# Weight-block sums moved from GpSimd to VectorE, two slices per tile, and more products kept for the end, in a two-layer mixture-of-experts kernel

## The chip, the cores and the metric

The kernel runs on one core of a Trainium2 chip. The metric is the device time of one execution in microseconds (us). TensorE is PE in the profile (PEld its weight loads), VectorE is DVE, ScalarE is ACT, GpSimd is POOL, and SP is the engine whose queue issues most DMAs.

## The reference, cut to what matters

Attention and a dense gated layer come first and yield x (2304 tokens x 512). Then each token goes to 2 of 8 experts:

```
out = zeros((2304, 512))
for e in range(8):
    for k in range(2):
        mask = top2[:, k] == e
        h = maximum(x[mask] @ w1[e], 0.0)                  # w1[e]: 512 x 1024
        out[mask] += top2_w[mask, k, None] * (h @ w2[e])   # w2[e]: 1024 x 512
```

All of it is fp32. The kernel gets that precision by splitting each operand into a rounded high part and a low rest, and using three matmuls per product (high x high, high x low, low x high). The high part is an ACT copy, the low part a DVE subtraction of two tiles in SBUF (the on-chip memory).

## The kernel before, in words

Three stretches follow each other. Up to some 435 us come attention and the dense layer (`slot1`), whose last block also routes the tokens and scatters their rows to DRAM, by expert. Then 32 *units* (some 435 to 549 us) do experts 0 and 1: `up2` is x @ w1 for one slice of 128 hidden columns, `down2` adds its product with w2 to accumulators in PSUM, one unit later. Part "a" of an expert is its first 384 rows, part "b" the rest. Units 12 to 15 are the second half of expert 1, part "a"; unit 16 starts its part "b". The rows of part "b" are loaded by SP (`load_x`, from unit 10 on, but only after the last scatters have landed), transposed by DVE (`trans_x`) and split (`split_x2`). `prep2` splits the weights of a unit two units ahead on ACT and DVE.

From 549 us on come 24 *pairs*, p = 0 to 23, four for each expert 2 to 7. A pair is two slices of w1 and w2. `pair` computes its x @ w1 by seven block products instead of eight (Winograd's form: A11, S2, A12, S3, S1, A22, S4 of the rows times blocks and sums of blocks of the weights); a product is six matmuls of 308 columns (`product`, L1058). The seven results are put together by DVE additions (`u2` L1096, `v` L1103, `y22` L1112, `y21` L1115, `y12` L1122), with ACT for `s1` and the relu, and DVE for the low parts (`split_low`, L1076). The matmuls of a pair with w2 (`down_s`, L1072: 5 row tiles x 2 slices x 3) are done in the next pair, between its products, by `first` and `second`.

For the next pair, each pair also prepares the weights. The raw blocks `wb` (512 KB a slice) stand in four buffers with the tag X1. `sums_ws` forms the sums of blocks, C and D, on GpSimd with four instructions of 256 columns (L1020 to L1023). `high_ws`/`low_ws` (L1038, L1042) split A, B, C and D; `high_w2`/`low_w2` (L1046, L1049) split the w2 part, once per slice. Rows of the next expert are prepared over its predecessor's four pairs: `load_xs` (L969), `trans_xs` (L981), `sums_xs` on GpSimd (L987 to L991), `high_xs`/`low_xs` (L1001, L1005).

The order of all this is written out by hand. `put` and `at` hang a piece of work on a stretch and a position in it; `run` emits all pieces up to a position. Each engine's queue is in order, so a waiting instruction holds all behind it on its engine. In pair p, `first(0)` follows position 1, `first(1)` position 3, `second(0)` and `second(1)` stand at the end (before positions 5 and 6.9).

At the end of an expert `finish` scales an accumulator (row tile t) and `add` adds it to `out` by an indirect DMA on POOL's queue. For the last expert `gather` reads the rows of `out` back in pair 23, `finish` adds on DVE (L928), and `add` scatters the sums; each scatter waits for the one before to land. In pair 23 some `down_s` matmuls of pair 22 are held back for the end (row tiles 3 and 4).

Of the kernel before, what the change touches and what calls it, by code (L numbers as in the profile page):

```python
# [24 lines left out]
E = 8  # L25
# [42 lines left out]
def moe_program(ctx, tc, phi, kv, q, wa, wgn, nz, wb, out):  # L68
# [298 lines left out]
    def places(first):  # L367


        def pt(tag, n, shape=()):  # L370
            pool = w1pool if tag[0] == "G" else wpool
            return pool.tile([128, *shape, 2, 2, 256], F32, tag=tag, name="pt", bufs=n)

        if first:
            t = [pt("X1", 4) for _ in range(4)] + [pt("GH", 2) for _ in range(2)] + [pt("GL", 2) for _ in range(2)]
# [636 lines left out]
    def sums_ws(p):  # L1012
        f0, f1 = WB[24 + 2 * p][:, :512], WB[25 + 2 * p][:, :512]
        if p:
            c, d = [pools["s2"].tile([128, DM], F32, tag=t, name="ts") for t in ("tc", "td")]
        else:
            c, d = ro_tile(), ro_tile()
        TS[p, "C"], TS[p, "D"] = c, d
        u, v = slice(0, 256), slice(256, 512)
        G.tensor_sub(c[:, u], f1[:, u], f0[:, u])  # L1020
        G.tensor_sub(c[:, v], f1[:, v], f1[:, u])
        G.tensor_sub(d[:, u], f1[:, v], c[:, u])
        G.tensor_sub(d[:, v], f0[:, v], d[:, u])  # L1023
# [20 lines left out]
    def high_w2(n):  # L1044
        W2[n] = wtile()
        A.activation(r(W2[n][:, 0]), WB[n][:, 512:], AF.Copy)  # L1046

    def low_w2(n):
        V.tensor_sub(r(W2[n][:, 1]), WB[n][:, 512:], W2[n][:, 0])  # L1049
# [12 lines left out]
    def down_s(p, n, tiles):
        e, f = 2 + p // 4, 2 * (p % 4) + n
        hh, hl = HS[p, n]
        w = W2[24 + 2 * p + n]
        for t in tiles:
            h = height(e, t)
            if f == 0:
                AC2[e, t] = bank((0, 1, 4, 2, 3)[t], [128, DM], "acc")
            o = slice(128 * t, 128 * t + h)  # L1070
            for m, (a, b) in enumerate(((hh, 0), (hh, 1), (hl, 0))):
                P.matmul(AC2[e, t][:h], r(a[:, o]), r(w[:, b]), start=(f == 0 and m == 0),  # L1072
                         stop=(f == NF2 - 1 and m == 2))
# [4 lines left out]
    def pair(p, first, second):  # L1078
        e = 2 + p // 4
        lo, hi = slice(0, HB), slice(HB, CAPS)  # L1080

        def temp(name):
            return pools["s2"].tile([128, HB], F32, tag=name, name=name)

        h0 = [act.tile([128, CAP], F32, tag=t, name="hs") for t in ("ah", "al")]
        HS[p, 0] = h0
        run(("s", p), 0)
# [37 lines left out]
        run(("s", p), 6.9)  # L1125
        split_low(h1[1][:, lo], y12, h1[0][:, lo])
# [25 lines left out]
    for n in range(4):  # L1152
        put(last, 2 * n + 3.5, load_wb, n)
# [40 lines left out]
    for k in range(4):  # L1194
        then_x(1, 4 + k, "a", 1, k, "b")
# [21 lines left out]
    then(2, 1, "b", 0.5, sums_ws, 0)  # L1217
# [3 lines left out]
    then(2, 6, "b", 2.2, high_w2, 24)  # L1221
# [4 lines left out]
    pairs = 4 * (E - 2)  # L1226
    for p in range(pairs):
        e, q = 2 + p // 4, p % 4
        n = 24 + 2 * p
        at(p, 0, high_w2, n + 1)  # L1230
        at(p, 0, low_w2, n)
        at(p, 1, load_wb, n + 4)
        at(p, 2, low_w2, n + 1)
        at(p, 3, load_wb, n + 5)
        if p + 1 < pairs:
            at(p, 0, sums_ws, p + 1)
            for h, g, k in ((1, 2, "A"), (3, 4, "B"), (3, 5, "C"), (5, 6, "D")):
                at(p, h, high_ws, p + 1, k)
                at(p, g, low_ws, p + 1, k)
            at(p, 6, high_w2, n + 2)  # L1240
        if e + 1 < E:
            if q == 0:
                at(p, 0, load_xs, e + 1)
            if q == 2:
                at(p, 5.5, index, e + 1, "ab")
            for h, fn, k, m in {0: ((5.1, trans_xs, 0, 0), (5.1, trans_xs, 0, 1), (6.1, sums_xs, 0, 0)),
                                1: ((1.1, high_xs, 0, 0), (2.1, low_xs, 0, 0), (1.2, high_xs, 0, 1),
                                    (2.2, low_xs, 0, 1), (3.1, high_xs, 0, 2), (4.1, low_xs, 0, 2),
                                    (4.2, sums_xs, 0, 1), (5.2, high_xs, 0, 3), (6.1, low_xs, 0, 3)),
                                2: ((2.1, trans_xs, 1, 0), (4.1, trans_xs, 1, 1), (5.2, sums_xs, 1, 0),  # L1250
                                    (5.2, high_xs, 1, 0), (6.1, low_xs, 1, 0)),
                                3: ((1.1, high_xs, 1, 1), (2.1, low_xs, 1, 1), (1.2, high_xs, 1, 2),
                                    (2.2, low_xs, 1, 2), (2.3, sums_xs, 1, 1), (5.2, high_xs, 1, 3),
                                    (6.1, low_xs, 1, 3))}[q]:
                at(p, h, fn, e + 1, k, m)
    then(2, 4, "b", 1, index, 2, "ab")
# [20 lines left out]
    for p in range(pairs):  # L1277
        e, q = 2 + p // 4, p % 4
        at(p, 2.5, add)
        at(p, 5.9, add)  # L1280
# [9 lines left out]
        else:  # L1290
            ends, held = q == 0, p == pairs - 1

            def first(h):
                down_s(p - 1, 0, (range(3), range(3, 3 if held else NC))[h])

            def second(h):
                t = (range(1), range(1, 3)) if held else (range(3), range(3, NC))
                down_s(p - 1, 1, t[h])
                if ends:
                    finish(e - 1, t[h])  # L1300
# [96 lines left out]
```

## Time and profile before

| what | us |
|---|---|
| median of 3 runs (lowest, highest) | 894.87 (894.37, 895.64) |
| the profiled execution | 897.11 |
| its span in the trace | 895.3 |
| PE busy, share | 837.7, 94% |
| PEld busy, share | 735.6, 82% |
| DVE busy, share | 644.1, 72% |
| ACT busy, share | 394.5, 44% |
| POOL busy, share | 336.1, 38% |

PE's busy time has modelled ends; idle time of PE is what the stretches, the waits and the timeline show.

### The profile page before, as it was taken

How to read it: one execution, taken by the hardware profiler on the slowest of the kernel's cores; microseconds unless marked ns; L12 is line 12 of the kernel's file. 1: busy time of each engine (PE TensorE's matmuls, PEld its weight loads, DVE VectorE, ACT ScalarE, POOL GpSimd, SP SyncE). 2: the span in 40 equal slices, each digit the busy share in tenths (PEclk: the TensorE clock that was granted, in tenths of full speed). 3: DMA queues.
4: the chain of work that ended last, by engine and by line, in shares of the span. 5: the costliest groups of instructions: out<-in, count | busy, mean ns of one | idle time of the engine just before them, and what ended most of it. 6: DMA issues, size and time to landing. Idle time of an engine off the chain costs nothing.

```text
span 895.3 us, 16500 instructions
## 1 busy us (share of the span) xinstructions
PE 837.7 (94%) x6136; PEld 735.6 (82%) x6136; DVE 644.1 (72%) x1498; ACT 394.5 (44%) x845; POOL 336.1 (38%) x443
## 2 busy tenths in 40 slices
PE   5898999999999999999997999899999999999992
PEld 2676888899989999898876878788888888888881
DVE  4786587776767685858673665788889989888751
ACT  4663555343443243334342544445454454544520
POOL 2000012424242333432223154545738557475622
PEclk9998999999999999999999999899999999999997
DMA  9965729875336443467466955455475645653431
GB/s 320 400 247 196 208 97 302 262 242 142 106 84 212 119 126 88 127 211 188 151 202 167 202 157 85 117 128 133 92 157 116 139 118 120 127 130 102 86 79 59
DMA packets 85082, 142.02 MB, mean 159 GB/s; under 512 B 16432, under 2 KB 41232, under 8 KB 84992
## 3 DMA queue, kind: packets, MB, share of 16 engines
q1 hardware_dynamic: 65712, 100.66, 36.8%
q0 software_dynamic: 19280, 40.22, 19.5%
q8 instruction: 50, 0.82, 0.4%
q14 instruction: 40, 0.33, 0.1%
HBM read 104.07 MB, written 36.77 MB: 157 GB/s over the span
## 4 chain that ended last, share of the span: by engine, by line
PE 65%; DVE 13%; DMA 11%; issue 5%; ACT 3%; POOL 1%; SPq 1%; DVEq 0%; POOLq 0%; ACTq 0%
PE acc L459 13%; PE acc L1072 12%; PE ph L1058 11%; PE pg L426 9%; PE pv L426 7%; DMA xs<-R,gidx 4%; PE ph L896 3%; PE acc L914 3%; PE acc L455 2%; PE pp L314 2%; DVE ws L1049 2%; DVE xh L1005 2%; DMA out<-pv,ix 1%; DVE ws L1042 1%; PE pT L481 1%
## 5 line engine op out<-in xcount | busy, mean ns | idle before, releaser
L1072 PE MATMUL acc<-ws,hs 128*128 128x512 f32 (+1 forms) x720 | 183.1, 396 | 0.0
L1058 PE MATMUL ph<-xh,ws 128*128 128x308 f32 x1008 | 165.0, 308 | 10.2 <-DVE ws L1042 4.4
L1058 PEld LDWEIGHTS ph<-xh,ws 128*128 128x128 f32 x1008 | 152.3, 189 | 25.7 <-DVE ws L1042 6.1
L1072 PEld LDWEIGHTS acc<-ws,hs 128*128 128x128 f32 (+1 forms) x720 | 129.5, 186 | 25.7
L459 PE MATMUL acc<-a,ro 128*128 128x288 f32 x576 | 116.3, 295 | 0.0
L426 PE MATMUL pg<-x,pt 128*128 128x288 f32 x576 | 103.9, 316 | 6.5 <-ACT pt L394 4.7
L459 PE MATMUL acc<-a,os 128*128 128x288 f32 x432 | 105.9, 294 | 0.8 <-DVE os L408 0.8
L938 POOL DMA_INDIRECT out<-pv,ix x40 | 65.1, 1629 | 109.0 <-ACT pv L931 57.9
L426 PEld LDWEIGHTS pg<-x,pt 128*128 128x128 f32 x576 | 83.0, 193 | 24.8 <-issue 6.2
L426 PE MATMUL pv<-x,pt 128*128 128x288 f32 x576 | 94.0, 299 | 0.0
L459 PEld LDWEIGHTS acc<-a,ro 128*128 128x128 f32 x576 | 92.2, 188 | 0.0
L439 DVE SCALAR_TENSOR_TENSOR ta<-ta,pg 128x288 f32<-128x288 f32 x84 | 37.8, 450 | 66.5 <-ACT ta L434 66.5
L426 PEld LDWEIGHTS pv<-x,pt 128*128 128x128 f32 x576 | 83.8, 193 | 0.0
L622 POOL DMA_INDIRECT xs<-R,gidx x48 | 49.0, 1021 | 88.4 <-DMA xs<-R,gidx 83.2
L418 POOL DMA_DIRECT2D os<-osl x72 | 40.6, 564 | 106.1 <-PE acc L459 62.0
L459 PEld LDWEIGHTS acc<-a,os 128*128 128x128 f32 x432 | 74.1, 189 | 1.1 <-DVE os L408 1.1
L434 ACT ACTIVATE ta<-pg 128x288 f32<-128x288 f32 x84 | 34.3, 408 | 88.4 <-PE pg L426 88.2
L445 ACT ACTIVATE a<-ta 128x288 fp32r<-128x288 f32 x84 | 37.3, 444 | 73.0 <-DVE ta L440 72.7
L896 PE MATMUL ph<-xt,wm 128*128 128x384 f32 (+1 forms) x256 | 59.1, 318 | 2.3 <-ACT xt L858 1.1
L1076 DVE SCALAR_TENSOR_TENSOR hs<-y,hs 128x308 fp32r<-128x308 f32 x72 | 50.9, 707 | 3.4 <-ACT hs L1123 0.5
L896 PEld LDWEIGHTS ph<-xt,wm 128*128 128x128 f32 x256 | 45.1, 193 | 6.6 <-ACT xt L858 2.2
L896 PE MATMUL ph<-xt,ro 128*128 128x384 f32 (+1 forms) x128 | 40.5, 317 | 5.2 <-DVE ro L779 5.1
(213 smaller groups left out, 1524.1 us busy)
## 6 DMA issues: line engine op xcount, KB each, us to landing
wb<-wb SPq DMA_DIRECT2D x72, 512.0 KB, 4.3
os<-osl POOLq DMA_DIRECT2D x72, 256.0 KB, 3.4
stg<-wa SPq DMA_DIRECT2D x19, 511.8 KB, 7.9
kv<-kv SPq DMA_DIRECT2D x32, 256.0 KB, 5.4
xl<-xs SPq DMA_DIRECT2D x40, 160.0 KB, 6.5
out<-zt SPq DMA_DIRECT2D x1, 5888.0 KB, 24.2
xd<-R SPq DMA_DIRECT2D x8, 603.0 KB, 4.8
qt<-q SPq DMA_DIRECT2D x8, 576.0 KB, 6.5
```

The lines of the kernel that those rows point to most:

```text
L418: G.dma_start(r(lo), r(osl[f][:, :]))
L426: P.matmul(p, r(PT[f // 2, g][:, w, f % 2, 128 * a:128 * a + 128]), r(X[i][:, s, g, :]), start=(g == 0 and n == 0), stop=(g == 1 and n == 2))
L434: A.activation(ta, pg, AF.Tanh, scale=0.5)
L439: V.scalar_tensor_tensor(ta, ta, 1.0, pg, op0=OP.add, op1=OP.mult)
L445: A.activation(r(ah[:, 0, :]), ta, AF.Copy)
L459: P.matmul(ACC[i][c], r(OS[i, f][w][:, o]), r(ah[:, s, :]), start=(f == 0 and n == 0), stop=(f == NF1 - 1 and n == 2))
L622: G.indirect_dma_start(out=xs[:, :], out_offset=bass.IndirectOffsetOnAxis(ap=RT[i][:, t, n:n + 1], axis=0), in_=R[i][:, t, :], in_offset=None)
L896: P.matmul(p, r(w[:, c]), r(x[:, k, b, :]), start=(m == 0), stop=(m == 11))
L938: G.indirect_dma_start(out=out, out_offset=bass.IndirectOffsetOnAxis(ap=IX[e][:h, t:t + 1], axis=0), in_=PV[e, t][:h], in_offset=None, com ...
L1058: P.matmul(out, r(w[:, i, c + 128 * k:c + 128 * k + 128]), r(x[:, m, k, a]), start=(start and n == 0), stop=(n == 5), skip_group_check=not ...
L1072: P.matmul(AC2[e, t][:h], r(a[:, o]), r(w[:, b]), start=(f == 0 and m == 0), stop=(f == NF2 - 1 and m == 2))
L1076: V.scalar_tensor_tensor(r(hl), y, 0.0, hh, op0=OP.max, op1=OP.subtract)
```

## The change

- The four X1 tiles become one tile with four slots; `wb` loads go to slot n % 4. The first four loads stand later in the last dense block.
- `sums_ws` runs on DVE: one subtraction of 512 columns and two of 256. Two stand at position 0 of a pair, the third at 2.
- C and D share a tile for the high and one for the low parts. `high_w2` and `low_w2` do both slices in one instruction; `low_w2` stands at position 2, and both `wb` loads at 3.
- The relu outputs of two slices share a tile: relu and `split_low` of the hi halves become one instruction of 616 columns each. `s1`, `u2` and the y of the hi halves stand in the tiles "ah" and "al".
- All positions of a pair run up to .9 (0.9, 1.9, ...), and there is one more: 6.9 before y12, 7.9 before its `split_low`.
- Rows: part "b" of expert 1 is transposed in units 13 to 15, not 12 to 15. `trans_xs`, `sums_xs`, `high_xs`, `low_xs` have other positions.
- `down_s` products kept for the end: in pair 22 only row tiles 0 and 1 of pair 21 are done, in pair 23 only tile 0 of pair 22. Operands of pair 23 go to an extra tile, KEEP.

```diff
@@ places / load_wb
-            t = [pt("X1", 4) for _ in range(4)] + ...
+            u = pt("X1", 1, (4,))
+            t = [u[:, k] for k in range(4)] + ...
-            WB[n] = wpool.tile([128, 1024], F32, tag="X1", name="wb", bufs=4)
+                WB["all"] = wpool.tile([128, 4, 1024], F32, tag="X1", name="wb", bufs=1)
+            WB[n] = WB["all"][:, n % 4]
@@ sums_ws
-        G.tensor_sub(c[:, u], f1[:, u], f0[:, u])
-        G.tensor_sub(c[:, v], f1[:, v], f1[:, u])
-        G.tensor_sub(d[:, u], f1[:, v], c[:, u])
-        G.tensor_sub(d[:, v], f0[:, v], d[:, u])
+            V.tensor_sub(TS[p][0].rearrange("p (a w) -> p a w", a=2),
+                         raw[:, 1, :DM].rearrange("p (a w) -> p a w", a=2), raw[:, :, u])
+        elif m == 1:
+            V.tensor_sub(TS[p][1][:, u], raw[:, 1, v], TS[p][0][:, u])
         else:
+            V.tensor_sub(TS[p][1][:, v], raw[:, 0, v], TS[p][1][:, u])
@@ high_w2, low_w2 (one call a pair)
+        A.activation(r(W2[p][0]), raw_of(p)[:, :, DM:], AF.Copy)
+        V.tensor_sub(r(W2[p][1]), raw_of(p)[:, :, DM:], W2[p][0])
@@ pair
-        A.activation(r(h1[0][:, hi]), y22, AF.Relu)
-        V.tensor_add(y21, b, s1)
-        A.activation(r(h0[0][:, hi]), y21, AF.Relu)
-        split_low(h1[1][:, hi], y22, h1[0][:, hi])
-        split_low(h0[1][:, hi], y21, h0[0][:, hi])
+        V.tensor_add(y[:, 0], b, s1)
+        A.activation(r(hh[:, :, hi]), y, AF.Relu)
         second(0)
-        run(("s", p), 5)
+        run(("s", p), 5.9)
+        split_low(hl[:, :, hi], y, hh[:, :, hi])
         product(p, c, S4, B22, False)
+        run(("s", p), 6.9)
         V.tensor_add(y12, c, u2)
-        A.activation(r(h1[0][:, lo]), y12, AF.Relu)
+        A.activation(r(hh[:, 1, lo]), y12, AF.Relu)
         second(1)
-        run(("s", p), 6.9)
-        split_low(h1[1][:, lo], y12, h1[0][:, lo])
+        run(("s", p), 7.9)
+        split_low(hl[:, 1, lo], y12, hh[:, 1, lo])
@@ order
-        put(last, 2 * n + 3.5, load_wb, n)
+        put(last, (9.5, 9.6, 11.5, 11.6)[n], load_wb, n)
-        then_x(1, 4 + k, "a", 1, k, "b")
+        put(("u", (13, 14, 14, 15)[k]), (2.2, 1, 2.2, 1)[k], trans_x, 1, k, "b")
+        put(("u", (14, 14, 15, 15)[k]), (0.5, 2.1, 0.5, 2.1)[k], split_x2, 1, k, "b")
-        at(p, 0, low_w2, n)
-        at(p, 1, load_wb, n + 4)
-        at(p, 2, low_w2, n + 1)
+        at(p, 2, low_w2, p)
+        at(p, 3, load_wb, n + 4)
         at(p, 3, load_wb, n + 5)
-            at(p, 0, sums_ws, p + 1)
-            for h, g, k in ((1, 2, "A"), (3, 4, "B"), (3, 5, "C"), (5, 6, "D")):
+            at(p, 0, sums_ws, p + 1, 0)
+            at(p, 0, sums_ws, p + 1, 1)
+            at(p, 2, sums_ws, p + 1, 2)
+            for h, g, k in ((1, 2, "A"), (3, 4, "B"), (3, 5, "C"), (4, 6, "D")):
-            for h, fn, k, m in {0: ((5.1, trans_xs, 0, 0), (5.1, trans_xs, 0, 1), (6.1, sums_xs, 0, 0)),
+            for h, fn, k, m in {0: ((6, trans_xs, 0, 0), (7, trans_xs, 0, 1)),
...
@@ end
+        held = max(0, p - pairs + 3)
+        inline = range((NC, 2, 1)[held])
+                down_s(p - 1, 0, inline[3 * h:3 * h + 3])
...
-    p = pairs - 1
-    down_s(p, 0, range(3))
+    rest = {t: [p for p in range(pairs - 3 + (t < 2) + (t < 1), pairs)] for t in range(NC)}
+    for n in range(2):
+        down_s(rest[1][0], n, (1,))
+    del rest[1][0]
     for t in range(NC):
-        if t > 2:
+        for p in rest[t]:
             for n in range(2):
-                down_s(p - 1, n, (t,))
-            down_s(p, 0, (t,))
-        down_s(p, 1, (t,))
+                down_s(p, n, (t,))
         finish(E - 1, (t,))
```

## Rows read from the trace of the kernel before

**Rows 1.** Busy time by stretch: stretch, length, engines with counts, granted clock, DMA share, GB/s.
```profile
549.00:573.00 24.00, 19.02 (x98) 16.50 (x97) 17.01 (x27) 10.06 (x21) 12.55 (x12) 0.86 0.74 165
...
600.00:654.00 54.00, 52.84 (x290) 45.88 (x289) 47.37 (x74) 27.40 (x57) 32.80 (x30) 1.00 0.59 131
```
**Rows 2.** The same view for two single pairs.
```profile
604.21:617.11 12.90, 12.90 (x73) 11.48 (x72) 9.64 (x18) 7.43 (x16) 3.86 (x3) 1.00 0.59 131
617.11:630.97 13.86, 13.42 (x74) 11.48 (x73) 13.44 (x21) 7.54 (x16) 10.17 (x9) 1.00 0.49 114
```
**Rows 3.** Waits of PEld, 573 to 856 us: waited for, us in total, times, longest.
```profile
PEld ph L1058 <- DVE u L1096: 5.7, 10, 0.7
PEld ph L1058 <- DVE v L1103: 3.4, 8, 0.6
```
**Rows 4.** DVE groups by form, 573 to 816 us (18 pairs): busy, mean ns, idle before.
```profile
L1076 DVE SCALAR_TENSOR_TENSOR hs<-y,hs 128x308 fp32r<-128x308 f32 x54 | 40.1, 742 | 2.1
L1049 DVE TENSOR_TENSOR ws<-wb,ws 128x512 fp32r<-128x512 f32 x36 | 35.5, 986 | 0.0
L1042 DVE TENSOR_TENSOR ws<-ts,ws 128x512 fp32r<-128x512 f32 x36 | 29.3, 813 | 0.0
L1042 DVE TENSOR_TENSOR ws<-wb,ws 128x512 fp32r<-128x512 f32 x18 | 18.7, 1041 | 0.0
...
L1042 DVE TENSOR_TENSOR ws<-wb,ws 128x256 fp32r<-128x256 f32 x18 | 7.8, 435 | 0.0
```
**Rows 5.** The same view, 856 to 896 us, where GpSimd computes nothing.
```profile
L1076 DVE SCALAR_TENSOR_TENSOR hs<-y,hs 128x308 fp32r<-128x308 f32 x5 | 2.4, 477 | 0.8 <-ACT hs L1123 0.5
L1049 DVE TENSOR_TENSOR ws<-wb,ws 128x512 fp32r<-128x512 f32 x2 | 1.4, 712 | 0.0
```
**Rows 6.** One of GpSimd's four groups of sums, 549 to 896 us.
```profile
L1022 POOL TENSOR_TENSOR ts<-wb,ts 128x256 f32<-128x256 f32 x23 | 29.9, 1302 | 3.5 <-DVE ws L1042 3.5
```
**Rows 7.** Timeline of the end: start, us, engine, line, operation, count [idle before, releaser].
```profile
867.68 11.26 PE L1072 MATMUL acc<-ws,hs 128*128 128x512 f32 x48
...
872.05 2.13 DVE L928 SCALAR_TENSOR_TENSOR pv<-acc,ml,pv 128x512 f32<-128x512 f32 x3 [2.68 <-PE acc L1072]
873.08 1.02 POOL L938 DMA_INDIRECT out<-pv,ix  x1 [8.26 <-DVE pv L928]
...
878.98 0.75 DVE L928 SCALAR_TENSOR_TENSOR pv<-acc,ml,pv 104x512 f32<-104x512 f32 x1 [2.02 <-PE acc L1072]
...
887.17 1.01 POOL L938 DMA_INDIRECT out<-pv,ix  x1 [2.59 <-DMA out<-pv,ix]
```
**Rows 8.** Timeline of units 14 and 15 (484 to 498 us), PE, DVE and SP.
```profile
484.49 1.80 SPq L844 DMA_DIRECT2D xl<-xs  x4
484.91 0.52 PE L896 MATMUL ph<-xt,wm 128*128 128x384 f32 x2
...
489.48 0.45 DVE L853 STREAM_TRANSPOSE xu<-xl 128x256 f32<-128x256 f32 x1 [9.49 <-DMA ml<-xs]
...
490.55 0.69 PE L896 MATMUL ph<-xt,ro 128*128 128x384 f32 x1 [5.13 <-DVE ro L779]
...
493.77 0.39 PE L914 MATMUL acc<-wm,hh 128*128 128x512 f32 x1
...
497.96 0.39 PE L914 MATMUL acc<-wm,hh 128*128 128x512 f32 x1
```
**Rows 9.** Timeline of pairs 0 and 1, PE and DVE.
```profile
548.80 1.84 PE L1058 MATMUL ph<-xh,ws 128*128 128x308 f32 x12
...
561.00 1.57 DVE L981 STREAM_TRANSPOSE xr<-xl 128x640 f32<-128x640 f32 x2 [1.92 <-issue]
...
563.20 1.40 PE L1058 MATMUL ph<-xh,ws 128*128 128x308 f32 x4 [4.38 <-DVE ws L1042]
...
571.53 1.86 PE L1058 MATMUL ph<-xh,ws 128*128 128x308 f32 x12
```
**Rows 10.** Loads of weight blocks (L765), 540 to 640 us, issue to landing.
```profile
DMA to landing us min/median/max: 3.1/4.3/7.4
```

More of the change, by code (lines that the diff above doesn't have):

```diff
@@ L374, in places @@
         if first:
-            t = [pt("X1", 4) for _ in range(4)] + [pt("GH", 2) for _ in range(2)] + [pt("GL", 2) for _ in range(2)]
+            u = pt("X1", 1, (4,))
+            t = [u[:, k] for k in range(4)] + [pt("GH", 2) for _ in range(2)] + [pt("GL", 2) for _ in range(2)]
         else:
@@ L763, in load_wb @@
         if n < len(STAGES) * NF2:
-            WB[n] = wpool.tile([128, 1024], F32, tag="X1", name="wb", bufs=4)
+            if "all" not in WB:
+                WB["all"] = wpool.tile([128, 4, 1024], F32, tag="X1", name="wb", bufs=1)
+            WB[n] = WB["all"][:, n % 4]
             Q.dma_start(WB[n], wb[STAGES[n // NF2], n % NF2])
@@ L1042, in low_ws, with high_w2, low_w2 @@
         V.tensor_sub(r(o), raw, h)
[L1044 to L1049, printed above, removed]
+    def high_w2(p):
+        if p == pairs - 1:
+            t = KEEP[:, 2 * 2 * CAPS:2 * 2 * CAPS + 4 * DM].rearrange("p (a f w) -> p a f w", a=2, f=2)
+            W2[p] = t[:, 0], t[:, 1]
+        else:
+            W2[p] = wtile(), wtile()
+        A.activation(r(W2[p][0]), raw_of(p)[:, :, DM:], AF.Copy)
+    def low_w2(p):
+        V.tensor_sub(r(W2[p][1]), raw_of(p)[:, :, DM:], W2[p][0])
     def product(p, out, a, b, start):
@@ L1063, in down_s @@
         e, f = 2 + p // 4, 2 * (p % 4) + n
-        hh, hl = HS[p, n]
-        w = W2[24 + 2 * p + n]
+        hh, hl = HS[p]
+        w = W2[p]
         for t in tiles:
@@ L1071, in down_s @@
             for m, (a, b) in enumerate(((hh, 0), (hh, 1), (hl, 0))):
-                P.matmul(AC2[e, t][:h], r(a[:, o]), r(w[:, b]), start=(f == 0 and m == 0),
+                P.matmul(AC2[e, t][:h], r(a[:, n, o]), r(w[b][:, n]), start=(f == 0 and m == 0),
                          stop=(f == NF2 - 1 and m == 2))
@@ L1080, in pair @@
         lo, hi = slice(0, HB), slice(HB, CAPS)
[L1082 to L1087, printed above, removed]
+        if p == pairs - 1:
+            t = KEEP[:, :4 * CAPS].rearrange("p (a f w) -> p a f w", a=2, f=2)
+            hh, hl = t[:, 0], t[:, 1]
+        else:
+            hh, hl = [pools["s2"].tile([128, 2, CAPS], F32, tag=t, name="hs", bufs=2) for t in ("hh", "hl")]
+        HS[p] = hh, hl
+        y, su = [act.tile([128, CAP], F32, tag=t, name="y")[:, :CAPS].rearrange("p (f w) -> p f w", f=2)
+                 for t in ("ah", "al")]
+        s1, u2 = su[:, 0], su[:, 1]
+        v, y12 = [pools["s2"].tile([128, HB], F32, tag=t, name=t) for t in ("v", "y12")]
+        run(("s", p), 0.9)
         a, b = bank(5, [128, HB], "ph"), bank(6, [128, HB], "ph")
@@ L1216, in moe_program @@
                 put(("u", f), h + 1.1, low_xs, 2, k, m)
-    then(2, 1, "b", 0.5, sums_ws, 0)
+    pairs = 4 * (E - 2)
+    for m in range(3):
+        then(2, 1, "b", 0.5, sums_ws, 0, m)
     for n in range(4):
@@ L1220, in moe_program @@
         then(2, 2 + n, "b", 2.2, low_ws, 0, "ADCB"[n])
-    then(2, 6, "b", 2.2, high_w2, 24)
+    then(2, 7, "b", 2.2, high_w2, 0)
+    then(2, 4, "b", 1, index, 2, "ab")
     def at(p, h, fn, *a):
         put(("s", p), h, fn, *a)
-    pairs = 4 * (E - 2)
     for p in range(pairs):
@@ L1279, in moe_program @@
         at(p, 2.5, add)
-        at(p, 5.9, add)
+        at(p, 6.5, add)
+        held = max(0, p - pairs + 3)
+        inline = range((NC, 2, 1)[held])
         if p == 0:
@@ L1290, in moe_program @@
         else:
-            ends, held = q == 0, p == pairs - 1
             def first(h):
-                down_s(p - 1, 0, (range(3), range(3, 3 if held else NC))[h])
+                down_s(p - 1, 0, inline[3 * h:3 * h + 3])
             def second(h):
[L1297 to L1300, printed above, removed]
+                t = inline[3 * h:3 * h + 3]
+                down_s(p - 1, 1, t)
+                if q == 0:
+                    finish(e - 1, t)
                     if h:
                         rows(e, "ab")
+        if p == pairs - 3:
+            KEEP = pools["s1"].tile([128, 2, 2, 7, HB], F32, tag="xs", name="keep").rearrange(
+                "p a k n w -> p (a k n w)")
         if p == pairs - 1:
```

81 lines of the change are left out of this document (41 added, 40 removed).

## The prediction, made before the result was known

> **What bounds the kernel now.** I read the shares first (PE is busy 94% of the span, DVE 72%), then busy time by stretch, and then, for the stretches that the change touches, who waits for whom and the timeline. The mean hides that PE is the bound nearly everywhere: in an expert of the pairs it is busy 52.84 of 54.00 us, at full clock [rows 1]. So an edit can only give back PE's stalls, or time after PE's last matmul. There are four such places.
>
> The price of matmuls first. The last 48 of w2 take 11.26 us [rows 7], 0.2346 each. A pair without a stall takes 12.90 us [rows 2] for 30 of them (7.04) and 42 of the products, so a product matmul is 5.86/42 = 0.1396.
>
> - Units 14 and 15: unit 15 shows what one costs, 497.96 - 493.77 = 4.19 us, of which 9 x 0.2346 = 2.11 are for w2 and 2.08 for `up2`. Unit 14's `up2` ran from 484.91 to 493.77, 8.86 us: a stall of 6.8. DVE stood 9.49 us for the rows of part "b", and behind it the weights ("ro") that unit 14 wanted [rows 8].
> - Pairs 0 and 1: from 548.80 to pair 1's fifth product at 571.53 are 22.73 us [rows 9]. The work there is 66 x 0.1396 + 21 x 0.2346 = 14.1, so 8.6 are stalls. DVE waits for the next expert's rows at 561.00, and the last weights of pair 1, D, stand behind that transpose: PE waits 4.38. The clock falls with it, to 0.86 over the stretch [rows 1].
> - Pairs after that: from 571.53 to 867.68 [rows 7, 9] are 296.15 us, the work 942 x 0.1396 + 657 x 0.2346 = 285.6. So 10.5 are stalls, half a us a pair. PEld names `u2` (5.7 us) and `v` (3.4) [rows 3]: DVE is late. It is busy 47.37 of 54 us, or 11.84 of a pair [rows 1].
> - The end: PE's last matmul ends at 867.68 + 11.26 = 878.94, the last sum soon after, but the last scatter starts at 887.17 [rows 7]. The five start (887.17 - 873.08)/4 = 3.52 us apart, each after the one before has landed. Row tiles 0 to 2 end in one burst; from there the chain of scatters is the bound, not PE.
>
> **The end, -7.0 us.** The matmuls are the same in number, but more of them now come last: tile 1 of pair 22 (6), tile 0 of pair 23 (6), tile 1 (6), then 18 for each of tiles 2 to 4. With E for PE's end, tiles 0 to 4 are ready 60, 54, 36, 18 and 0 matmuls before E: at E-14.1, -12.7, -8.4, -4.2 and 0. From a tile's last matmul to its scatter were 1.18 us (871.90, 18 matmuls after 867.68, to 873.08). With the 3.52 apart they start at -12.9, -9.4, -5.9, -2.3, and the last at E+1.2; before at E+8.2. What precedes the burst: pairs 22 and 23 lose PE work (42 x 0.1396 + 12 x 0.2346 = 8.7 and, with 6 for w2, 7.3 us are left), and pair 22 has DVE work for pair 23 still. DVE's chain there is about as long, so I add 0.7 (0 to 2) as a new stall.
>
> **Units 14 to 16, -3.8 us.** The rows land when they did, at 489.48, since the scatters and SP's load stay. But the first transpose now stands behind the weights of units 14 and 15. PE can work until unit 16, the first that reads the rows, at 484.91 + 2 x 4.19 = 493.3. From 489.48 on DVE has 8 instructions of 256 columns (0.45, [rows 8]), two low parts and four weight splits of about 0.71 [rows 5]: 7.9 us, so the last rows come at some 497.4. Unit 16 could have ended near 494.8; it ends three matmuls after 497.4. Of 6.8 some 3 are left. Bounds: all goes (-6.8), or the ACT copies between stretch the chain (-1.5).
>
> **Pairs 0 and 1, -4.3 us.** Low D now precedes the transposes (6 and 7), so pair 1's second product doesn't wait for rows. What is late next: `u2` of pair 1 stands behind both transposes, y12, `split_low` and the sums for pair 2. With rows at 561.0 that is 561.0 + 1.57 + 2 x 0.48 + 0.71 + 0.44, or about 564.7, and PE wants it about 563.3. With 0.9 for D, and 1.1 lost in pair 0 (`u2` there stands behind two sums that wait for the pool to open), and a little for `v`, I count 4.3 of 8.6 as left. Bounds: -6 to 0 (the low clock may stay).
>
> **The pairs between, -6 us.** This is the sums' part, and the least sure. DVE gets 0.71 + 2 x 0.435 = 1.58 us a pair more [rows 4, 5]. It saves two instructions by merging; the fixed part of one is 2 x 0.435 - 0.712 = 0.16, so 0.32. And its own instructions that read two tiles in SBUF are slow while GpSimd computes: 986 against 712 ns, 742 against 477 [rows 4, 5]. Over 18 pairs the excess is 36 x 0.274 + 36 x 0.101 + 18 x 0.329 + 54 x 0.265 = 33.7 us, 1.9 a pair. GpSimd's sums take up to 1.3 us each [rows 6], four a pair; those of the rows, which stay, are two a pair. So I give the former two thirds, 1.3. Net 0: DVE stays at some 11.8 of 12.9.
>
> So the load hardly moves. What moves is the order. Before, `u2` stood behind one or two slow splits (a w2 split at 0.99, row parts that waited for GpSimd); now behind two sums (1.15 together) with nothing contending in most pairs, and the w2 split follows it. PE wants `u2` 9 w2 and 6 product matmuls after its input is complete, 2.9 us: enough, if DVE reaches the sums by then. `v` has 6 and 6, 2.2 us; between `u2` and it stand the w2 split of both slices (2 x 0.712 - 0.16 = 1.26), a sum (0.44) and low A (0.71), which end before `v`'s input does. I let 4.5 of the 10.5 stay. Bounds: -10.5 (no stall) and +5 (0.2 a pair).
>
> The new wait: at position 0 DVE, no longer GpSimd, waits for the raw blocks of the next pair, with `u2` behind it. They are now both asked for after `low_w2`, about 3.5 us into a pair, and wanted about 13; two loads of 3.1 to 7.4 [rows 10] fit one behind the other but for the worst. The merged load of SP also passes before the rows of an expert, as now. The other edits cost nothing: the shared tiles move no work, and the first loads, four slots of the dense block later, still have three of them before use.
>
> What speaks against this step: the rows have GpSimd and DVE hindering one another, 986 against 712 ns [rows 4, 5]. The Trainium skill, "Perfetto Trace Analysis", section "Optimizing Scalar/DVE Operations", says that they share an SBUF read port, so that moving work from one to the other might not help. The rows agree that they get in each other's way, but the hindrance there is GpSimd's and should go with its sums. If nothing went, DVE would have 11.84 + 1.26 = 13.1 us in a pair of 12.9, and would be the bound; by the rows it is level.
>
> Sum: 7.0 - 0.7 + 3.8 + 4.3 + 6 = 20.4 us. Made on the profiled execution (897.11) it is 876.7; that one is 2.2 above the median (894.87), so I forecast 874.5.
>
> **The rivals.** (1) *Moving the sums buys nothing* (26%): DVE's load is level by the sum above, and with the sums ahead of `u2` the stalls stay at 10.5 or grow by 5; the ramp gives back only 2. For it: 11.8 of 12.9 leaves little slack for any order. Against: the waits are 0.5 to 0.7 us each [rows 3], small against 1 to 2 us that leave DVE's queue ahead of `u2`. The time: 894.9 - 6.3 - 3.8 - 2 = 882.8, or 888 with the 5, where DVE at 13.1 us a pair is the bound and the old misfit of 0.5 comes on top of it in half of the pairs. This is what the page named above warns of.
>
> (2) *Slower: DVE waits for weights* (6%). The loop is load, sums, `u2`, `low_w2`, next load: 1.15 + 0.5 + 1.3 us and the landing of two blocks. It decides once both land later than 12.9 - 2.9 = 10 us after issue; at 11.5 each pair loses 1.5, 33 us over 22, against 10 to 11 from the end and the units: 917. For it: 7.4 for one block [rows 10], and one pair in four loads rows too. Against: the median of 4.3, and blocks can land side by side.
>
> (3) *The change doesn't do what it says* (2%): slots of one tile wait for each other as if they were the whole, so that a load holds the splits of the other slots. It would cost some 2 us in each of 22 pairs, less the end: near 925. The output rows of the kernel before already share one tile, and no wait in the rows is of that kind.
>
> (4) Small gains and small losses cancel, 895 (3%).
>
> **How the numbers follow.** 63% for the forecast, whose own range is 866 to 880. To 888 the range takes in rival 1 with its worst; below, -7 - 6.8 - 6 - 10.5 gives 865. Something like 0.2% (1.8 us) is what a measurement can tell from no change. Faster: 63 + 26, so 0.89; same 0.03; slower 0.08.
>
> **What would show it.** Right: the last scatter starts within 2 us of the last sum; PE's stall in unit 14 is gone, with some 3 us in unit 16; PE doesn't wait for low D in pair 1; DVE's 512-column splits come near 0.7 us; PEld's waits for `u2` and `v` halve; GpSimd is free of L1020 to L1023. Wrong: DVE waits at the sums for wb; PEld's waits for DVE in the pairs stay at 9 us or more; pairs 22 and 23 give back more than 2 us.

## The result and the profile after

The kernel after takes 882.09 us (median of 4 runs, 881.52 to 883.97), the kernel before on the same chip 895.25 (894.37 to 896.88): ratio 0.9855 [0.9833, 0.9876]. That is 13.2 us faster, inside the forecast's range (865 to 888), but 7.6 us short of its 874.5 and nearest to rival 1 (882.8). The profiled execution took 881.73 us, its span 879.9.

Measured with the landmarks of the prediction, the two profiled executions (897.11 and 881.73) differ by 15.4 us:

| stretch | before | after | difference | forecast |
|---|---|---|---|---|
| start to unit 14's first matmul | 484.91 | 482.30 | -2.6 | 0 |
| units 14 to 31, to pair 0's first product | 63.89 | 61.56 | -2.3 | -3.8 |
| to pair 1's fifth product | 22.73 | 23.01 | +0.3 | -4.3 |
| to the last product of pair 23, less its matmuls | 10.5 | 0.5 | -10.0 | -6 |
| PE's last matmul to the span's end | 16.36 | 15.73 | -0.6 | -7.0 + 0.7 |

The first row is not the change: the difference is there by the first matmul of L285 (96.38 and 93.78 us), in code that is the same in both. The before profile lay 1.9 us above the median of 895.25. In the fourth row the matmuls at the prices of the prediction are taken off, so it holds stalls alone: 24 matmuls with w2 moved behind the last product and are no gain.

**The pairs.** The busy times by stretch (core 0; length, engines, granted clock, DMA share, GB/s) that answer to [rows 1], and PEld's waits (573 to 845 us) that answer to [rows 3]. Pair 0 begins 4.9 us earlier here than before, so the first row doesn't hold quite the same work:

```profile
550.00:573.00 23.00, 19.03 (x89) 15.72 (x88) 17.94 (x32) 8.35 (x16) 5.30 (x5) 0.85 0.60 153
600.00:654.00 54.00, 54.00 (x301) 47.88 (x301) 47.05 (x82) 27.26 (x51) 17.18 (x13) 1.00 0.57 129
```
```profile
PEld ph L1075 <- ACT y L1112: 0.7, 1, 0.7
```
PE is busy 54.00 of 54 us (52.84 before); the 9.1 us of PEld's waits for `u2` and `v` are gone altogether. Between pair 1's fifth product (566.87) and the end of pair 23's last (847.32 by its count of matmuls) lie 280.45 us; 942 products and 633 w2 matmuls at the prices of the prediction are 280.0. DVE's load has hardly moved, 47.05 us for 47.37. Its groups by form, 573 to 816 us (busy, mean ns):

```profile
L1055 DVE TENSOR_TENSOR ws<-ts,ws 128x512 fp32r<-128x512 f32 x38 | 28.6, 753 | 0.0
L1066 DVE TENSOR_TENSOR ws<-wb,ws 128x1024 fp32r<-128x1024 f32 x19 | 23.1, 1213 | 0.0
L1028 DVE TENSOR_TENSOR ts<-wb 128x512 f32<-128x512 f32 x19 | 19.0, 998 | 0.0
...
L1055 DVE TENSOR_TENSOR ws<-wb,ws 128x512 fp32r<-128x512 f32 x19 | 13.0, 685 | 0.0
```
The 512-column splits take 685 and 753 ns (1041 and 813 in [rows 4]), both w2 halves 1213 (2 x 986). In their place stand the sums; the first of them, also 512 columns, takes 998.

**Pairs 0 and 1.** Timeline rows of PE, DVE and ACT (start, duration, [idle before, releaser]), answering to [rows 9]:

```profile
554.83 0.83 PE L1075 MATMUL ph<-xh,ws 128*128 128x308 f32 x4 [0.53 <-DVE ws L1055]
...
560.63 3.88 PE L1075 MATMUL ph<-xh,ws 128*128 128x308 f32 x12 [2.87 <-ACT y L1112]
```
```profile
557.61 0.84 DVE L984 STREAM_TRANSPOSE xr<-xl 128x640 f32<-128x640 f32 x1 [2.83 <-issue]
558.38 0.44 DVE L1136 TENSOR_TENSOR y<-ph,y 128x308 f32<-128x308 f32 x1
```
```profile
558.85 0.46 ACT L1137 ACTIVATE hs<-y 128x308 fp32r<-128x308 f32 x1 [5.51 <-DVE y L1136]
559.22 1.04 ACT L1063 ACTIVATE ws<-wb 128x1024 fp32r<-128x1024 f32 x1
560.16 0.41 ACT L1112 ACTIVATE y<-ph 128x308 f32<-128x308 f32 x1
```
Low D is no longer late (0.53 us; 4.38 before), but the stall is not smaller: DVE's transpose still waits 2.83 us for the rows (its row names no releaser; in the trace of the kernel before the last of these loads lands at 560.9, and the transpose starts at 561.00), `y12` stands behind it, ACT's relu behind `y12`, and behind the relu stand a weight copy and `s1`, without which PE can't go on. The matmuls after the wait run at half the clock: 12 in 3.88 us (1.85 where PE had not waited). Read a queue through to its end: one late transpose held two engines. `u2` is late as well. In pair 0 PE waits 0.55 us for it, and in the profile of the repeat (the first experiment below) PE waits in pair 1 first for `s1` and then for `u2`, which on DVE stands behind the first two sums:

```profile
558.70 1.11 PE L1075 MATMUL ph<-xh,ws 128*128 128x308 f32 x6 [2.73 <-ACT y L1112]
560.68 1.88 PE L1075 MATMUL ph<-xh,ws 128*128 128x308 f32 x6 [0.87 <-DVE y L1115]
```

**The end.** POOL's indirect DMAs and PE's last matmuls, answering to [rows 7]:

```profile
836.31 1.55 POOL L941 DMA_INDIRECT out<-pv,ix  x1 [3.84 <-ACT ws L1051]
842.00 1.61 POOL L941 DMA_INDIRECT out<-pv,ix  x1 [4.14 <-ACT keep L1063]
847.61 1.33 POOL L947 DMA_INDIRECT pv<-out,ix  x1 [4.00 <-DMA out<-pv,ix]
...
853.08 1.00 POOL L947 DMA_INDIRECT pv<-out,ix  x1 [0.30 <-issue]
857.71 1.02 POOL L941 DMA_INDIRECT out<-pv,ix  x1 [3.63 <-DMA pv<-out,ix]
...
872.03 1.01 POOL L941 DMA_INDIRECT out<-pv,ix  x1 [2.59 <-DMA out<-pv,ix]
```
```profile
862.64 1.53 PE L1089 MATMUL acc<-keep 128*104 128x512 f32 x6
```
PE ends at E = 864.17. The last scatter starts at E+7.9 (before E+8.2). The first starts at E-6.5, not at E-12.9: it waits for a gather, the gathers for the last `add` of expert 6, and the five adds start 815.81 to 842.00, 5.5 to 9.2 us apart. Two of the rows above name an ACT instruction as the releaser; the trace has the add of 830.80 landing at 835.56, 0.75 us before the next one starts, and shows the same 0.75 us in the profiles of seven other runs, so I read the adds as a chain too. I had looked at who waits for PE at the end, and not at what POOL's queue had ahead of the gathers.

### The profile page after: what moved, and what is told of

It reads as the page before. It is cut to its first block, busy times and chain, and to the rows that moved or that the text cites. A ratio compares the mean times of both kernels' runs of the same rounds, so it can differ in the third digit from the quotient of the medians.

```text
span 879.9 us, 16299 instructions
## 1 busy us (share of the span) xinstructions
PE 832.4 (95%) x6136; PEld 733.4 (83%) x6136; DVE 635.0 (72%) x1522; ACT 389.1 (44%) x797; POOL 244.1 (28%) x347
## 4 chain that ended last, share of the span: by engine, by line
PE 77%; DVE 9%; DMA 8%; ACT 2%; issue 2%; SPq 1%; POOL 0%; POOLq 0%; DVEq 0%; ACTq 0%
PE acc L1089 19%; PE ph L1075 15%; PE acc L460 13%; PE pg L427 9%; PE pv L427 7%; DMA xs<-R,gidx 4%; PE acc L917 3%; PE ph L899 3%; PE pp L314 2%; PE acc L456 2%; PE pkv L285 1%; DMA wb<-wb 1%; DMA out<-pv,ix 1%; PE pT L482 1%; PE psc L314 1%
## 5 line engine op out<-in xcount | busy, mean ns | idle before, releaser
L1089 PE MATMUL acc<-ws,hs 128*128 128x512 f32 (+1 forms) x690 | 176.1, 396 | 0.0
L1075 PE MATMUL ph<-xh,ws 128*128 128x308 f32 x1008 | 160.1, 306 | 4.8 <-ACT y L1112 3.1
L1089 PEld LDWEIGHTS acc<-ws,hs 128*128 128x128 f32 (+1 forms) x690 | 123.4, 185 | 24.6
L941 POOL DMA_INDIRECT out<-pv,ix x40 | 68.6, 1714 | 188.8 <-ACT pv L934 93.6
L441 DVE TENSOR_TENSOR ta<-ta,pv 128x288 f32<-128x288 f32 x84 | 38.2, 455 | 8.8
L447 DVE TENSOR_TENSOR a<-ta,a 128x288 fp32r<-128x288 f32 x84 | 37.4, 445 | 6.7 <-ACT a L446 6.3
```

Of the source, the lines that this page charges most:

```text
L441: V.tensor_mul(ta, ta, pv)
L447: V.tensor_sub(r(ah[:, 1, :]), ta, ah[:, 0, :])
L941: G.indirect_dma_start(out=out, out_offset=bass.IndirectOffsetOnAxis(ap=IX[e][:h, t:t + 1], axis=0), in_=PV[e, t][:h], in_offset=None, com ...
L1075: P.matmul(out, r(w[i][:, c + 128 * k:c + 128 * k + 128]), r(x[:, m, k, a]), start=(start and n == 0), stop=(n == 5), skip_group_check=not ...
L1089: P.matmul(AC2[e, t][:h], r(a[:, n, o]), r(w[b][:, n]), start=(f == 0 and m == 0), stop=(f == NF2 - 1 and m == 2))
```

## Experiments

They ran in three sets of four, each set on one chip together with the kernel before (medians 896.11, 895.46 and 896.07); the ratios are to these. A stretch or a wait is read from one profiled execution of each kernel.

**The kernel after again.**


> The changed kernel once more, to have it beside the others on one chip: 882 us, ratio to before 0.985. Every other run of this call is read against it.


Measured: 881.96 us, ratio 0.9854 [0.9833, 0.9876].

**The sums back on GpSimd, all else as after.**
```diff
-            V.tensor_sub(TS[p][0].rearrange("p (a w) -> p a w", a=2),
-                         raw[:, 1, :DM].rearrange("p (a w) -> p a w", a=2), raw[:, :, u])
+            G.tensor_sub(TS[p][0][:, u], raw[:, 1, u], raw[:, 0, u])
+            G.tensor_sub(TS[p][0][:, v], raw[:, 1, v], raw[:, 1, u])
...
-            V.tensor_sub(TS[p][1]...      # twice
+            G.tensor_sub(TS[p][1]...
```


> The changed kernel with the sums of weight blocks back on GpSimd (the four instructions of before), all else as changed. Theory (GpSimd's sums made DVE late by slowing its two-input instructions): the 512-column low parts go back from near 0.7 to near 0.95 us, PE's stalls between pair 1 and pair 22 come back from 0.5 us to 6 to 10 us, and the run takes 6 to 10 us more than the changed kernel, 888 to 892. Rival (the order and the merged instructions did it): stalls stay below 3 us, 882 to 885.


Measured: 876.95 us, 0.9803 [0.9775, 0.983]. My theory missed, and of its rival the mechanism held (no stalls) but not the time: the step of the title that moves the sums to VectorE is not needed for the gain and rather costs 5 us. The same DVE view, and the stretch:

```profile
L1066 DVE TENSOR_TENSOR ws<-wb,ws 128x1024 fp32r<-128x1024 f32 x19 | 30.4, 1600 | 0.0
...
L1055 DVE TENSOR_TENSOR ws<-wb,ws 128x512 fp32r<-128x512 f32 x19 | 21.9, 1155 | 0.0
```
```profile
600.00:654.00 54.00, 54.00 (x303) 47.98 (x302) 45.96 (x68) 26.42 (x50) 34.02 (x30) 1.00 0.57 127
```
With GpSimd at work the splits are slow again (1155 for 685 ns, 1600 for 1213), as the hindrance of the prediction says, and yet PE is busy 54.00 us and DVE 45.96, 0.4 to 1.1 less than with the sums (46.37 in the repeat of after, 47.05 in after). So the relief was real and paid for what DVE took over, and it was not the cause of the gain. The Trainium skill, "Perfetto Trace Analysis", section "Optimizing Scalar/DVE Operations", warns that moving work between these two engines might not help, as they share a port; the two loads, 47.05 and 45.96, agree.

Pairs 0 and 1 differ too, and this bears on the forecast of 4.3 us there. From pair 0's first product to pair 1's fifth this kernel takes 19.94 us. The six other profiles with the sums on VectorE and the transposes at after's places have 22.3 to 23.2.

```profile
547.64 5.91 PE L1075 MATMUL ph<-xh,ws 128*128 128x308 f32 x38
...
559.78 2.95 PE L1075 MATMUL ph<-xh,ws 128*128 128x308 f32 x12 [2.64 <-ACT y L1112]
```
PE waits for `s1` as in after, but not for `u2`, in neither pair: here no sums stand ahead of it on DVE. About half of this is lost again by the last product (281.9 us for 280.45).

Where the 5 us lie, by profile: POOL's last indirect DMAs, to set beside those of after.

```profile
839.65 1.61 POOL L941 DMA_INDIRECT out<-pv,ix  x1 [3.37 <-DMA out<-pv,ix]
844.75 1.03 POOL L947 DMA_INDIRECT pv<-out,ix  x1 [3.49 <-DMA out<-pv,ix]
...
868.44 1.01 POOL L941 DMA_INDIRECT out<-pv,ix  x1 [2.59 <-DMA out<-pv,ix]
```
By the ends of their records the last product ends at 846.56 here, 847.48 in after; the last scatter starts 21.9 us later, in after 24.6. The adds follow each other somewhat faster (815 to 845 in 29.8 us, 31.8 in after). Another 1.5 lies between the last scatter's start and the span's end (6.4 for 7.9), where no row shows why. Why the adds are faster is not settled.

**The kernel before with only the sums on VectorE.**
```diff
-        G.tensor_sub(...)   # four times, at position 0
+        V.tensor_sub(...)
```


> The kernel before with one edit: its four sums of weight blocks are issued on DVE in place of GpSimd (position 0, behind the w2 split). Theory (GpSimd's sums slow DVE): DVE's 512-column low parts fall from 0.95 to about 0.7 us, stalls in the pairs from 10.5 to 2 to 6, 5 to 8 us less, 887 to 890. Rival (the order matters: now u2 stands behind 0.6 us of w2 split and 1.5 us of sums): stalls as before or more, 894 to 899.


Measured: 893.45 us, 0.997 [0.9955, 0.9985]: 2 to 3 us, between the two forecasts and nearer to the rival's. The w2 splits fell from 986 to 755 ns, and PE still waited for `u2` twice in four pairs.

**The kernel before with the order of after alone.**
```diff
-        at(p, 0, low_w2, n)
-        at(p, 1, load_wb, n + 4)
+        at(p, 2, low_w2, n)
+        at(p, 3, load_wb, n + 4)
...              # and trans_xs, sums_xs, high_xs, low_xs at the places of after, as 6.1, 6.2 for 7, 7.1
```


> The kernel before with VectorE's order of the kernel after alone: the first half of the split of w2 behind u2, and the row parts at the new kernel's places. Nothing merged, sums on GpSimd, the end as before. Theory (order): PE's stalls between the pairs were waits for u2 and v behind too much work at one place; PE is busy 241 us or more of the 243 from 573 to 816 (237.8 before), time 886 to 889. Rival (merging, fewer and longer instructions): 239 or less, 893 to 897.


Measured: 890.13 us, 0.9944 [0.992, 0.9968], between the two forecasts. The stretch that I had named, 573 to 816, shows 237.93, which would speak for the rival; but it holds one wait of 2.4 us in the ramp (pair 2, for weights):

```profile
575.58 0.83 PE L1058 MATMUL ph<-xh,ws 128*128 128x308 f32 x4 [2.43 <-DVE ws L1042]
```
So I took another measure, chosen after the result: the period of four pairs (one expert) in the steady part, read from PE's product that comes at the same place one expert later. Two rows each of before, of this kernel and of after:

```profile
690.03 1.11 PE L1058 MATMUL ph<-xh,ws 128*128 128x308 f32 x6 [0.31 <-DVE u L1096]
...
744.07 1.12 PE L1058 MATMUL ph<-xh,ws 128*128 128x308 f32 x6 [0.29 <-DVE u L1096]
```
```profile
634.32 1.12 PE L1058 MATMUL ph<-xh,ws 128*128 128x308 f32 x6 [0.35 <-DVE v L1103]
...
686.61 1.10 PE L1058 MATMUL ph<-xh,ws 128*128 128x308 f32 x6 [0.56 <-DVE v L1103]
```
```profile
609.35 1.01 PE L1075 MATMUL ph<-xh,ws 128*128 128x308 f32 x6
...
660.91 1.01 PE L1075 MATMUL ph<-xh,ws 128*128 128x308 f32 x6
```

| kernel | period of 4 pairs, us | of the 2.5 us lost, gone |
|---|---|---|
| before | 54.04 | |
| before, sums on DVE | 53.2 | 0.8 |
| before, order of after | 52.29 | 1.75 |
| after, sums on GpSimd | 51.57 | 2.5 |
| after | 51.56 | 2.5 |

The order alone gives 70% of it. The whole way from pair 0's first product to the end of pair 23's last points the same way (5.63 us added where 24 matmuls of w2 come later): 318.9 us before, 316.7 with the sums on VectorE, 310.4 with the order alone, 309.1 after, 307.5 after with the sums on GpSimd. The profiled execution of the order alone was the fastest of its seven (887.18 us, 3 below the median), so its share of the whole, 8.5 of 9.8, may be somewhat high. All waits for `u2` are gone; one wait for `v` in four pairs is left, where the w2 split still comes in two slow halves (1195 ns each). The order together with the merged instructions, sums on GpSimd, gives all.

**The kernel after with the order of before.**
```diff
-        at(p, 2, low_w2, p)
+        at(p, 0, low_w2, p)
...              # and the row parts at the places of before
```


> The kernel after with VectorE's order of the kernel before: the split of w2 ahead of u2 and the row parts at the old places; merged instructions, sums on VectorE and the end as after. Theory (order): the stalls come back, three a period of four pairs, PE busy 239 us or less of the 243 from 573 to 816, time 888 to 894. Rival (merging): 242 or more, 881 to 885.


Measured: 888.38 us, 0.9912 [0.9886, 0.9937], as the order theory said, PE busy 237.89 of 243. But it shows less than I meant it to: the wait is for another reason.

```profile
617.73 1.23 DVE L1066 TENSOR_TENSOR ws<-wb,ws 128x1024 fp32r<-128x1024 f32 x1 [1.62 <-ACT ws L1063]
```
At position 0 the merged split waits for ACT's copy of both slices, which comes at the end of the pair before. The old place and the merged copy don't go together; the test before this one is the clean one.

**The products held as before.** `inline` and `rest` as in the kernel before, all else as after.


> The changed kernel with the products kept for the end as before (only tiles 3 and 4 of pair 22). Theory (the chain at the end hangs on the gathers, which hang on the adds of expert 6, so holding more products back moved nothing): same within 1 us as the changed kernel, 881 to 883; the last scatter starts about 8 us after PE's last matmul. Rival (the held products gave their 7 us and something else lost it): 7 us more, 889.


Measured: 882.7 us, 0.9847 [0.983, 0.9863], as the theory said. Holding more products bought nothing by itself.

**Gathers moved ahead.**
```diff
-            if e == E - 1:
+            if e >= E - 2:        # finish: expert 6 too sums on DVE and scatters
...
-        if p == pairs - 1:
+        if p == pairs - 5:
+            at(p, 0.1, gather, E - 2)
+        if p == pairs - 3:
             at(p, 2.6, gather, E - 1)
```


> The changed kernel, but expert 6 too reads its rows of the output back in pair 19 and scatters sums (as the last expert does) in place of five accumulating adds, and the last expert's gather is asked for in pair 21. Theory (adds of 5.6 us, then gathers, then scatters are the bound at the end): the gathers have landed before row tile 0 is ready, the first scatter starts about 13 us ahead of PE's end and the last 1 to 2 us behind it; 6 to 7 us less, 875 to 876. Rival (the scatters wait for something else, or DVE's five more sums in pair 20 stall PE): 880 to 884.


Measured: 875.55 us, 0.977 [0.9752, 0.9788], 6.4 less than after. Its end, PE ending at 862.09 + 1.53 = 863.62:

```profile
842.59 1.62 POOL L947 DMA_INDIRECT pv<-out,ix  x1 [0.31 <-issue]
850.79 1.02 POOL L941 DMA_INDIRECT out<-pv,ix  x1 [6.58 <-DVE pv L931]
...
865.25 1.01 POOL L941 DMA_INDIRECT out<-pv,ix  x1 [2.96 <-DVE pv L931]
```
The last gather goes out at 842.59 and nothing waits for it. The first scatter starts at E-12.8 and waits for DVE's sum; the last at E+1.6. The prediction had E-12.9 and E+1.2: with the gathers out of the way the held products do what I forecast for them. The edit does two things, sums in place of adds for expert 6 and an earlier last gather, and it has the held products; which of these is needed was not tried one by one.

**Both: gathers ahead and sums on GpSimd.** The two edits above together.


> The kernel after, with the sums of weight blocks back on GpSimd and the outputs of expert 6 gathered in pair 19 too (the last gather in pair 21). Theory: with the sums on GpSimd the only gain lay at the end, where the accumulating scatters of expert 6 and the gathers behind them came 1.8 to 2.8 us sooner against PE; with the gathers moved ahead nothing waits for them, so this run is within 1.5 us of the one with the gathers alone (875.5): 874 to 877, first scatter on a wait for DVE's sum. Rival: GpSimd's sums unload DVE all along and the two gains add: 870 to 872.


Measured: 889.12 us, 0.992 [0.9894, 0.9946], 13 us worse than expected, so neither theory. PE, ACT and POOL about 840 us:

```profile
840.80 0.88 PE L1075 MATMUL ph<-xh,ws 128*128 128x308 f32 x2 [6.68 <-ACT ws L1051]
```
```profile
838.15 0.63 ACT L1051 ACTIVATE ws<-ts 128x512 fp32r<-128x512 f32 x1 [12.32 <-POOL ts L1029]
```
```profile
831.35 0.96 POOL L941 DMA_INDIRECT out<-pv,ix  x1 [5.30 <-DMA out<-pv,ix]
835.67 1.01 POOL L941 DMA_INDIRECT out<-pv,ix  x1 [3.36 <-DMA out<-pv,ix]
836.71 0.73 POOL L1028 TENSOR_TENSOR ts<-wb 128x256 f32<-128x256 f32 x1
```
Each scatter waits on POOL for the one before to land, and the weight sums of the next pair stand behind the whole chain: ACT stands 12.3 us, PE 6.7. Shorter waits for the same weights (1.65 us at 808, 1.16 at 843) and a granted clock of 0.81 from 835 to 862 come on top. In this arrangement sums on DVE pay: they keep the weights out of a queue that waits for DMAs. But `finish` puts the five scatters of expert 6 into the queue at one place, where the adds that they replace stand half a pair apart with the sums between them. Scatters spread like the adds, with the sums on GpSimd, were not run, and could do as well as sums on DVE.

**That, with expert 3's transposes in pair 1 behind `u2`.** The edit of the next but one, added.


> As the first of these runs, with expert 3's transposes moved into pair 1 behind u2. That alone took 3.3 us from the stretch from pair 0's first product to pair 1's fifth (23.01 to 19.68) and no time from the whole. Theory: the whole waited for the scatters and gathers of the end; with these gone ahead, the 3 us show: 871 to 874. Rival: what is saved there is lost in the pairs behind it (v late, 0.6): 874 to 877.


Measured: 886.07 us, 0.988 [0.9854, 0.9906]. The same stall of 6.9 us at 840; 3 us less than without the transposes' move, just at the edge of what the intervals tell apart. Pairs 0 and 1, up to the fifth product, take 15.50 us here for 14.1 of work: with neither the transposes nor the sums ahead of `u2` the stall there is all but gone.

**Rows of part "b" at the old places.**
```diff
-        put(("u", (13, 14, 14, 15)[k]), (2.2, 1, 2.2, 1)[k], trans_x, 1, k, "b")
-        put(("u", (14, 14, 15, 15)[k]), (0.5, 2.1, 0.5, 2.1)[k], split_x2, 1, k, "b")
+        then_x(1, 4 + k, "a", 1, k, "b")
```


> The changed kernel with the rows of part b of expert 1 transposed and split in units 12 to 15 as before. Theory (the transpose at the head of DVE's queue held the weights of unit 14; moving it gave 2.3 us between unit 14 and the first pair): PE's stall of 5 us in unit 14 comes back, the run takes 2 to 3 us more than the changed kernel, 884 to 885. Rival (the start of part b is bound by the rows' arrival whatever the order): within 1 us, 881 to 883.


Measured: 884.53 us, 0.9872 [0.9844, 0.9901], as the theory said, though the interval overlaps that of after. Unit 14 waits 3.89 us for its weights again. In after it doesn't wait; unit 16 does, 2.9 us in five waits, the longest of them in the last row here (the first row is this run's, the others are after's):

```profile
488.76 0.44 PE L899 MATMUL ph<-xt,ro 128*128 128x384 f32 x1 [3.89 <-DVE ro L782]
```
```profile
491.21 0.69 DVE L782 TENSOR_TENSOR ro<-wb,wm 128x512 fp32r<-128x512 f32 x1 [1.97 <-ACT wm L781]
...
492.89 0.38 PE L899 MATMUL ph<-xt,wm 128*128 128x256 f32 x1 [0.98 <-DVE xt L862]
```
From 92 us (the first matmul of L285) to pair 0's first product the four kernels with the old places take 452.4 to 453.8 us, the nine with the new 449.4 to 452.0 (the kernel with other places, next but one, left out). The step is worth some 2.4 us (means 453.0 and 450.6).

**The transposes of expert 3 late.** In pair 1, `trans_xs` at 2.05 and 2.06 in place of pair 0's 6 and 7, and the row parts after them.


> The changed kernel, but for expert 3 alone the rows' transposes go from the end of pair 0 into pair 1, behind u2, and what follows from them half a pair later. Theory (y12 of pair 0 stood behind the transpose on DVE, its relu held ACT, and with it s1 of pair 1: 2.9 us of PE's wait and a low clock after it): the wait for s1 in pair 1 is gone, pairs 0 and 1 lose 4 to 5 us less, 877 to 878. Rival (the weights' arrival or DVE's backlog takes its place): within 1.5 us, 880.5 to 883.


Measured: 881.43 us, 0.9836 [0.9809, 0.9863]; no gain. DVE and PE in pair 1:

```profile
561.15 0.69 DVE L1028 TENSOR_TENSOR ts<-wb 128x512 f32<-128x512 f32 x1 [3.43 <-DMA wb<-wb]
```
```profile
562.74 1.11 PE L1075 MATMUL ph<-xh,ws 128*128 128x308 f32 x6 [2.58 <-DVE y L1115]
```
The rows are out of the way and DVE now waits as long for the next weights. Still pair 0's first product to pair 1's fifth fell from 23.01 to 19.68 us, and the clock stayed at 1.00 there (0.85 in after). In this profile pair 0 began 1.5 us later and the last scatter 0.25 earlier than in after.

**Rows of part "b" closer together.** `trans_x` and `split_x2` all in units 13 and 14.


> The changed kernel, but all four transposes and splits of part b stand ahead of the weight split of unit 14, whose load is late. Theory (in unit 16 the rows came late since ACT stood waiting for a weight block ahead of their split): PE's waits for the rows in unit 16 fall from 4 us to about 1, 2 to 4 us less, 878 to 880. Rival (DVE's chain of eight instructions is as long in any order): within 1 us.


Measured: 885.54 us, 0.9872 [0.9839, 0.9904], no gain. In its profile unit 16 has hardly a wait for rows, but a stall stands 20 us on, where ACT's relu is behind a weight copy that waits 6.7 us for its block's load, issued behind the next rows:

```profile
516.48 0.50 PE L917 MATMUL acc<-wm,hh 128*128 128x512 f32 x1 [3.19 <-ACT hh L902]
...
518.63 0.80 PE L917 MATMUL acc<-wm,hl 128*128 128x512 f32 x1 [1.42 <-DVE hl L903]
```
The kernel after has no such wait in its profile; that of its repeat has 2.1 us of waits for `hl`, the first at 514, and the kernel before 2.2.

The fastest of all is the kernel after with the gathers ahead, 875.55 us. With the transposes late as well, and sums on VectorE, it was not run.

## Why the prediction was right, and where not

- **The end, -7.0: failed, -0.6 measured.** The failed step is "they start at -12.9": it took the gathered rows as there. They come at E-6.5, behind the adds of expert 6, and the chain of scatters starts that much later. Moving the gathers brings 6.4 us, all that was missing. The new stall of 0.7 didn't come: pairs 22 and 23 lose nothing but 0.3.
- **Units 14 to 16, -3.8: mechanism right, size -2.4** (bounds -6.8 to -1.5). Unit 14 doesn't wait any more, unit 16 waits 2.9 us in the profile, and the stretch around it runs at a granted clock of 0.70 (492 to 500). The mis-sized term is the chain of DVE, put at 7.9 us without a wait in it: DVE waits 1.97 us for an ACT copy at 491.21, and that copy itself waited 1.81 us for its weight block to land.
- **Pairs 0 and 1, -4.3: failed, +0.3.** "PE doesn't wait for low D" held. "What is late next: `u2`" named only the second of two: first comes `s1` on ACT, behind the relu of a `y12` that stands behind the transposes, which the sum left out. Of 8.6 us it let 4.3 stay (its named terms, 1.4, 0.9 and 1.1, make 3.4, and the rest is more than "a little for `v`"); 8.9 stayed. `u2` is late too, behind the sums: take the sums off VectorE and 3 us go (19.94 us, and 19.98 in the run with the gathers ahead, for 23.01), take the transposes away and 3.3 go (19.68), take both and 7.5 go (15.50). With the transposes away and the sums on VectorE the sums wait for the next weights to land, the new wait that the prediction had expected to fit.
- **The pairs between, -6: right in cause, short in size, -10.0.** "The load hardly moves. What moves is the order" is what the runs show: loads 47.4, 47.05 and 45.96 us, and 70% of the steady gain with the order alone; the rest came with the merged instructions. Merging alone was not tried. "This is the sums' part" was wrong: moving the sums was not needed for it. I let 4.5 of 10.5 stay for safety; 0.5 stayed. The relief of DVE was about as said, 685 to 753 ns in place of 813 to 1041, and is not what removes the stalls in after, since they are gone without it.
- **The rivals.** Rival 1 came out near the measured time for other reasons: it wanted the pairs' stalls to stay and the end to gain. In its narrower sense, that moving the sums buys nothing, it is right for after (876.95 without, 881.96 with). Rival 2: DVE waits for weights only in the ramp. Rival 3: no wait between slots of one tile; its 925 should by its own terms be some 932, on which nothing hangs.

So it is luck that the total lies inside the range and only 7.6 us off: errors of one sign (the end and the ramp, 10.3 us too hopeful together, and the units 1.5) met one of the other (the pairs, 4).

## What to carry to other kernels

An engine at 85 to 90% load can cost the bound engine 2.5 us in 54 or nothing, and here the order of its queue made 70% of the difference: put what the bound engine wants next ahead of what has a pair's time left, then count the load. Before forecasting a chain, follow each of its inputs back to the start of its own chain, on the queue that issues it; here a scatter needed a gather that needed five adds. And keep work that others wait for out of a queue whose DMAs wait for one another.

## What the runs showed of the hardware

- An accumulating scatter of a row tile follows the one before by 5.5 to 5.8 us (836.31, 842.00 in after), a plain one by 3.5 (868.48, 872.03), where each waits for the one before. One such step took 9.2 us in after (821.61 to 830.80), while two weight blocks were being loaded, and with plain scatters 6.5 at the same place (821.99 to 828.51 with the gathers ahead). That the loads are the cause was not tried.
- A GpSimd subtraction of 256 columns takes 0.72 to 0.75 us where DVE waits (836.71 above) and 1.16 to 1.34 us on average in the pairs of after with the sums on GpSimd, so the hindrance of the two engines seems to go both ways; neighbouring GpSimd records overlap in part, so the average is rough.
- PE's granted clock fell after one wait and not after another of nearly the same length. The same stretch of pair 1 in after, behind PE's wait of 2.87 us, and in the kernel with the late transposes, where the wait of 2.58 us lies in it:

```profile
561.00:566.50 5.50, 5.43 (x18) 4.44 (x18) 5.46 (x11) 3.43 (x8) 0.88 (x1) 0.50 0.29 109
```
```profile
561.00:566.50 5.50, 3.34 (x18) 2.77 (x18) 5.32 (x9) 1.27 (x3) 0.11 (x1) 1.00 0.38 97
```
Both do 18 matmuls; the granted clock is 0.50 in the one, the lower level (1.2 GHz), and 1.00 in the other (2.4 GHz), so the first needs 5.43 us of PE and the second 3.34. In the repeat of after, 6 matmuls right behind the wait of 2.73 us take 1.11 us and the 6 behind the next wait 1.88 (rows above). What decides between them was not tried.
